# The first 26 and the last 40 microseconds of a layernorm–attention–SwiGLU kernel, put in another order

## Chip, cores and metric

The kernel runs on one core of a Trainium2 chip. The metric is the device time of one execution in microseconds (us). Times are given as the median of several runs; a profile is one execution more, taken by the hardware profiler, with a time of its own.

## What is computed

The input is x, 2048 rows of 512 numbers in float32. The reference, cut to what matters:

```python
xn = _layernorm(x, axis=-1)               # eps 1e-5
qkv = xn @ wqkv                           # H = 32 heads of Dh = 16
p = softmax(einsum(q, k) * Dh ** -0.5)    # 2048 x 2048 for each head
s = einsum(p, v) @ wo
b = (silu(xn @ w_gate) * (xn @ w_up)) @ w_down   # F = 1792
out = x + s * silu(b)
```

## The kernel before

**Precision.** A large product is made from three products: each operand is split into a rounded high part (a copy into the type fp32r) and the rest (a subtraction), and high·high, low·high and high·low are summed. So each operand costs a cast and a subtraction on its way, and each product three matmuls. Softmax weights times values alone run in plain float32.

**Opening and projections (L431 to L676).** The rows come in 4 blocks of 512 (`b`), each of 4 tiles of 128 rows (`t`). For one tile: `stats` (L501, L502) takes mean and variance, `rates` (L506 to L512) the reciprocal root, with one Newton step after ScalarE's square root, `norm` (L516) subtracts and multiplies into `xn`, and `turn_x` (L518 to L528) turns the tile by four transposes on TensorE into a bank `acc`, from which ScalarE copies the high part (L524) and VectorE makes the low one (L525). `load_w` and `split_w` (L461, L469, L470) bring a piece of wqkv and split it: ScalarE casts, GpSimd subtracts. In block 0 the four `value_tile`s come first (12 matmuls each, L538), then the eight `feature_tile`s (q and k, L536); in the later blocks the features come first. Before the first value tile stand: tile 0 in full, the four value weights' splits, then the statistics, rates and norms of the tiles 1 to 3 together. The list `slots` and the conditions on `n` in the loop after it set what is issued between the tiles. Each engine runs its own instructions in the order in which the program issues them.

**Attention (L740 to L777).** 32 units (`u`: 8 groups of 4 heads by 4 blocks of queries) of 8 steps each; the number of the step is `now`. In a step: 8 score matmuls, 4 exponentials on ScalarE (L749), and the value matmuls of the step before (L360). Between them `share` hands out a part of a queue of filler matmuls (L171): the whole feed-forward network of the 4 blocks (`ffn`), then the output projections (`project_out`): the one of block 3 with three of the four pieces of the attention output, then those of blocks 0, 1 and 2. They use the banks `bankx` and `banky`, each over 64 of the 128 rows of the array, and VectorE empties these two banks after each tile (for an output projection L330, L331); GpSimd then multiplies by the gate, adds x and stores (L332 to L334).

**Attention output.** `finish` normalises a unit; after every second group a turned piece `o2` goes to a scratch tensor in HBM (`o_d`, L382). `out_steps` plans, by `now` and by the length of the queue, when the pieces come back (`load_out`, L274), when they are split (`split_o`, L257, L258), and when the gates and rows of x are loaded (`load_gates`). The dictionary `stage` keeps what has been done; a projection of block b may start only when `(b, 3)` is in it, that is, when its last piece has been split. `load_gate` and `gate_rest` (L350, L351: four multiplications and four additions on VectorE) prepare the rows of block 3 in steps 248 and 251.

**The end (L778 to L801).** After the last values, block 3 of the last unit is normalised in two halves, turned, and split into `hi` and `lo`. `fill(total)` issues the 12 matmuls that remain of the projections (row tile number `end` = 11, into half of `score[0]`, L321). Then come four products with three matmuls each (L798) into the four banks of `outs`, a multiplication by the gate (L799), an addition (L800) and a store (L801) each.

Of the kernel before, what the change touches and what calls it, by code (L numbers as in the profile page):

```python
# [46 lines left out]
def tile_block(ctx: ExitStack, tc: tile.TileContext, x, wqkv, wo, w_gate, w_up, w_down, out):  # L47
# [237 lines left out]
    stage = {}  # L285
    splits = []

    def out_steps():
        for _ in range(min(2, len(splits))):
            b, c = splits.pop(0)  # L290
            split_o(lhs[b, c], parts_o[b, c])
            if c == DT - 1:
                stage[b, 3] = now
        for b in range(NB - 1):
# [10 lines left out]
            if (b, 1) in stage and (b, 5) not in stage and now > stage[b, 1]:  # L305
                splits.append((b, DT - 1))
                stage[b, 5] = now
            if len(queue) <= NB - 1 - b and (b, 4) not in stage:
                load_gates(b)
                stage[b, 4] = now  # L310

    def project_out(b, n=DT):
        catch_up()
        for j in range(NT):
            t = b * NT + j
            i = 0
            for c in range(n):
                for a, w in ((0, 0), (0, 1), (1, 0)):
                    lo, hi = lhs[b, c][a][:, j * P:(j + 1) * P], fx[:, w, c]
                    if t == end:  # L320
                        mm(score[0][:, 1], lo, hi, start=i == 0, stop=i == 3 * n - 1)  # L321
# [3 lines left out]
                    if i == 3 * n and n == DT:  # L325
                        y = two.tile([P, D], F32, tag="th", name="y")
                        if t == end:
                            act(y, score[0][:, 1], AF.Copy, scale=0.5)
# [3 lines left out]
                        pool.tensor_mul(y, y, gt[t])  # L332
                        pool.tensor_add(xr[t], y, xr[t])
                        (sp if t == end else pool).dma_start(out[rows[t]], xr[t])  # L334
# [66 lines left out]
    def fill(n):  # L401
        nonlocal given, left
        while n > 0 and queue and (queue[0][0] is None or (queue[0][0], 3) in stage):
# [25 lines left out]
    with ExitStack() as pro:  # L429
# [8 lines left out]

        def load_x(b):
            for t in range(NT):  # L440
                r = b * TB + t * P
                sp.dma_start(xin[:, t], x[r:r + P])

        load_x(0)
# [28 lines left out]
        for m in worder[:5]:  # L473
            load_w(m)
# [29 lines left out]
        def rates(first, last):  # L504
# [13 lines left out]
        def turn_x(b, t):  # L518
# [5 lines left out]
            nc.scalar.copy(hi, av)  # L524
            dve.tensor_sub(lo, av, hi.bitcast(F32))  # L525
# [4 lines left out]
        def project(pairs, xh, xl, tokens):  # L530
            ps = pps.tile([P, 512], F32, tag="ps", name="ps")
            n = 0
            for whi, wlo, c in pairs:
                for a, w in ((xh, whi), (xl, whi), (xh, wlo)):
# [41 lines left out]
        def value_tile(b, t):  # L576
            xh, xl = xt[b % 2]
            ps = project([(vh[:, c], vl[:, c], c) for c in range(DT)], xh, xl, slice(t * P, (t + 1) * P))
# [247 lines left out]
```

## Time and profile before

| | us |
|---|---|
| median of 3 runs | 1464.09 (1462.9 to 1464.17) |
| the profiled execution, its own time | 1465.16 |
| its span, first to last instruction | 1463.4 |
| TensorE busy with matmuls | 1440.6 |
| ScalarE busy | 1094.6 |
| VectorE busy | 536.0 |
| GpSimd busy | 91.2 |

The profile names engines PE (TensorE matmuls), PEld (its weight loads), DVE (VectorE), ACT (ScalarE), POOL (GpSimd) and SP (the queue that issues most DMAs). A row of the timeline has the start and the length in us, the engine, the line, the operation, the tiles written and read, their shapes and how often; in brackets, how long the engine was idle before it and what released it. A row of the windows view has a stretch, its length, the busy time of the engines, then the granted TensorE clock (1.00 is full speed), the share of time in which the DMA engines were busy, and what they moved in GB/s. Matmul ends are modelled, so the pitch from one start to the next is the safer measure.

### The profile page before, as it was taken

The page shows a single profiled execution, that of the slowest core. Times are in us where ns is not written, and L with a number is a line of the kernel's source. Part 1 is how long each engine was busy: PE and PEld are TensorE (multiplying, and loading weights), DVE is VectorE, ACT ScalarE, POOL GpSimd, SP SyncE. Part 2 cuts the span into 40 slices and gives each one's busy share as a digit, 9 for nine tenths or more (in the row PEclk, how much of TensorE's full clock was granted, in tenths as well). Part 3 has the DMA queues.
Part 4 walks back from the last instruction along what each step waited for, and adds up shares of the span by engine and source line. Part 5 has one row for each costly group of instructions (what it writes and reads, how often), then busy time and mean ns, then how long its engine had stood idle before and what let it go on. Part 6 is the DMA issues. An engine that isn't in the chain of part 4 may idle for free.

```text
span 1463.4 us, 26699 instructions
## 1 busy us (share of the span) xinstructions
PE 1440.6 (98%) x11213; PEld 803.8 (55%) x11213; DVE 536.0 (37%) x883; ACT 1094.6 (75%) x1218; POOL 91.2 (6%) x108
## 2 busy tenths in 40 slices
PE   7999999999999999999999999999999999999997
PEld 5777655555555555555555555555555555555553
DVE  5543343124333432244233423342334214334444
ACT  4433488788878887888788878887888778877773
POOL 3200200000000000000000000000000000000244
PEclk9999999999999999999999999999999999999999
DMA  7799652033273431143714401448144203313351
GB/s 254 267 288 296 166 120 61 12 88 88 69 173 79 92 77 34 45 103 81 166 42 108 99 12 40 101 94 182 35 98 107 55 12 69 93 52 127 114 193 73
DMA packets 130066, 155.94 MB, mean 107 GB/s; under 512 B 12764, under 2 KB 79324, under 8 KB 128916
## 3 DMA queue, kind: packets, MB, share of 16 engines
q1 hardware_dynamic: 124372, 131.17, 36.1%
q0 software_dynamic: 5280, 22.48, 4.1%
q8 instruction: 90, 1.47, 0.4%
q10 hardware_dynamic: 288, 0.52, 0.1%
q14 instruction: 36, 0.29, 0.1%
HBM read 111.66 MB, written 42.47 MB: 105 GB/s over the span
## 4 chain that ended last, share of the span: by engine, by line
PE 95%; DVE 2%; ACT 2%; DMA 1%; issue 1%; DVEq 0%; ACTq 0%
PE acc L360 32%; PE bankx L171 29%; PE score L747 20%; PE ps L536 5%; PE banky L171 5%; PE ps L538 3%; ACT pr L749 1%; DMA q_d<-parts 1%; PE acc L521 1%; DVE facc L350 0%; DMA facc<-in_A_x_dram 0%; DVE y L799 0%; DVE st L501 0%; DVE y L800 0%; PE score L798 0%
## 5 line engine op out<-in xcount | busy, mean ns | idle before, releaser
L749 ACT ACTIVATE pr<-score 128x1024 f32<-128x1024 f32 x1024 | 992.4, 1023 | 240.3 <-PE score L747 237.6
L360 PE MATMUL acc<-pr,vst 128*17 128x512 f32 x4096 | 490.0, 596 | 0.0
L747 PE MATMUL score<-qst,kst 50*128 50x512 f32 x2048 | 360.8, 424 | 2.8 <-ACT pr L749 2.0
L747 PEld LDWEIGHTS score<-qst,kst 50*128 50x128 f32 x2048 | 178.2, 185 | 273.1 <-ACT pr L749 235.6
L171 PE MATMUL bankx<-fx,guh 64*128 64x512 f32 x896 | 288.4, 392 | 0.0
L171 PE MATMUL banky<-fx,guh 64*128 64x512 f32 x896 | 288.3, 392 | 0.0
L360 PEld LDWEIGHTS acc<-pr,vst 128*17 128x17 f32 x4096 | 94.0, 96 | 236.5 <-issue 235.7
L199 DVE SCALAR_TENSOR_TENSOR ga<-th,bankx 128x512 f32<-128x512 f32 x56 | 38.5, 688 | 463.5 <-ACT th L198 463.5
L171 PEld LDWEIGHTS bankx<-fx,guh 64*128 64x128 f32 x896 | 165.8, 185 | 32.6 <-issue 0.3
L171 PE MATMUL bankx<-fx,gul 64*128 64x512 f32 x448 | 175.4, 391 | 0.0
L171 PE MATMUL banky<-fx,gul 64*128 64x512 f32 x448 | 175.3, 391 | 0.0
L171 PEld LDWEIGHTS banky<-fx,guh 64*128 64x128 f32 x896 | 165.7, 185 | 4.1
L171 PE MATMUL bankx<-wd,hh 64*128 64x512 f32 x672 | 165.8, 389 | 0.0
L171 PE MATMUL banky<-wd,hh 64*128 64x512 f32 x672 | 165.6, 388 | 0.0
L171 PEld LDWEIGHTS bankx<-wd,hh 64*128 64x128 f32 x672 | 124.0, 184 | 24.8
L171 PEld LDWEIGHTS banky<-wd,hh 64*128 64x128 f32 x672 | 124.0, 184 | 2.2
L171 PEld LDWEIGHTS bankx<-fx,gul 64*128 64x128 f32 x448 | 82.9, 185 | 17.5
L171 PEld LDWEIGHTS banky<-fx,gul 64*128 64x128 f32 x448 | 82.8, 185 | 1.8
L536 PE MATMUL ps<-xt,wh 128*128 128x512 f32 x256 | 80.9, 397 | 0.0
L131 DVE TENSOR_TENSOR gul<-gur,guh 128x1024 fp32r<-128x1024 f32 x56 | 68.6, 1225 | 2.1
L218 DVE COPY facc<-bankx 128x512 f32<-128x512 f32 x16 | 11.1, 692 | 131.0 <-PE banky L171 103.9
L382 POOL DMA_DIRECT2D o_d<-o x12 | 6.5, 545 | 820.7 <-DVE o L381 623.0
(138 smaller groups left out, 1050.5 us busy)
## 6 DMA issues: line engine op xcount, KB each, us to landing
fx<-xt_d SPq DMA_DIRECT2D x32, 512.0 KB
gur<-in_B_w_gate_dram SPq DMA_DIRECT2D x56, 256.0 KB
gur<-in_B_w_up_dram SPq DMA_DIRECT2D x56, 256.0 KB
wdr<-in_B_w_down_dram SPq DMA_DIRECT2D x56, 256.0 KB
kst<-k_d SPq DMA_DIRECT2D x192, 64.0 KB
qst<-q_d SPq DMA_DIRECT2D x192, 64.0 KB
xt_d<-xt POOLq DMA_DIRECT2D x8, 1024.0 KB, 6.2
q_d<-parts SPq DMA_DIRECT2D x16, 512.0 KB
```

The costliest lines, as they stand in the source:

```text
L131: dve.tensor_sub(lo, raw, hi.bitcast(F32))
L171: mm(bank, lhs[h], rhs[h], start=start, stop=stop)
L199: dve.scalar_tensor_tensor(ga, th, 1.0, bankx, op0=ALU.add, op1=ALU.mult)
L218: dve.tensor_copy(facc[:, t], bankx)
L360: mm(a[h * 32:h * 32 + DH + 1], v[:, kt % CT, h * (DH + 1):(h + 1) * (DH + 1)], probs[2 * i + h // 2][:, h % 2], start=kt == 0, stop=kt == ...
L382: (pool if g < NG - 1 else sp).dma_start(o_d[g // 2, b], o2)
L521: nc.tensor.transpose(a[:, c * P:(c + 1) * P], xn[t][:, c * P:(c + 1) * P], ident)
L536: mm(ps, w, a[:, c], start=n == 0, stop=n == 3 * DT - 1)
L538: mm(ps, a[:, c, tokens], w, start=n == 0, stop=n == 3 * DT - 1)
L747: mm(score[j][:, h], k[r, j, kc * P:(kc + 1) * P], q[r, j], start=True, stop=True)
L749: exps.append(act(pr, score[j], AF.Exp, scale=0.25))
```

## The change

Three places change; the matmuls of the 256 steps of attention stay as they are and in their order.

*Opening.* Twelve plain float32 matmuls of the identity with itself go to the bank `acc[1]` before any other work on TensorE. The loads come in the order x0, w8, x1, w9, w10, w11, x2, x3, w0 (before: x0 to x3, then w8 to w11 and w0). `rates` uses scalar operands: where three products of two tensors stood, each row tile has one operation with two scalar operands and one with one. The splits of w8 and w9 are issued ahead of the copies of tile 0, the statistics of tile 1 between its two copies, and tile 1 is normalised by itself. Value tile 0 takes all eight products with the high weights first, then two of the four with the low weights, then the transposes of row tile 1, then the other two; the other value tiles of block 0 take the products with `xl` last. The tiles 2 and 3 are normalised and turned after value tile 1. The loads of block 1 are issued one slot later.

*Attention output.* For the blocks 1 and 2 the last piece no longer goes through HBM: `finish` splits `o2` at once into slots of `wd` or `hh`. A counter `ready` takes the place of `(b, 3)`. For block 0 the last piece's split goes to the front of the list.

*End.* `fill(total)` stands ahead of the last normalisation; row tile 11 goes to `bankx`, and its evacuation (ScalarE) and its GpSimd work are issued after the first half of the last unit. Row tile 10 is stored from the SP queue instead of GpSimd's. `outs[2]` is `banky` instead of the other half of `score[1]`; the second low part is issued after the second product; all additions are on VectorE, and the stores alternate between the SP and the ScalarE queue.

```diff
+    ready = [0] * NB
...
             split_o(lhs[b, c], parts_o[b, c])
-            if c == DT - 1:
-                stage[b, 3] = now
+            ready[b] += 1
...
-            if b in stage and (b, 1) not in stage and now > (u0 + b) * steps:
+            if b in stage and not b and (b, 1) not in stage and now > (u0 + b) * steps:
...
-                splits.append((b, DT - 1))
+                splits.insert(0, (b, DT - 1))
...
+    def store_out(t, y):
+        pool.tensor_mul(y, y, gt[t])
+        pool.tensor_add(xr[t], y, xr[t])
+        (pool if t < end - 1 else sp).dma_start(out[rows[t]], xr[t])
...
-                        mm(score[0][:, 1], lo, hi, start=i == 0, stop=i == 3 * n - 1)
+                        mm(bankx, lo, hi, start=i == 0, stop=i == 3 * n - 1)
...
-                            act(y, score[0][:, 1], AF.Copy, scale=0.5)
+                            after.append(partial(act, y, bankx, AF.Copy, scale=0.5))
+                            after.append(partial(store_out, t, y))
...
-            (pool if g < NG - 1 else sp).dma_start(o_d[g // 2, b], o2)
+            if g < NG - 1 or not b:
+                (pool if g < NG - 1 else sp).dma_start(o_d[g // 2, b], o2)
+            else:
+                whole = (wd, hh)[b - 1].rearrange("p f j t -> p (f j) t")
+                lhs[b, DT - 1] = whole[:, 2 * (DT - 1)], whole[:, 2 * DT - 1]
+                split_o(lhs[b, DT - 1], o2)
+                ready[b] += 1
...
-        load_x(0)
...
-        for m in worder[:5]:
-            load_w(m)
+
+        for _ in range(12):
+            mm(acc[1][:, :P], ident, ident, start=True, stop=True)
+        for kind, i in ((load_tile, 0), (load_w, 8), (load_tile, 1), (load_w, 9), (load_w, 10), (load_w, 11),
+                        (load_tile, 2), (load_tile, 3), (load_w, 0)):
+            kind(i)
...
-            dve.tensor_mul(n, r, r)
-            dve.tensor_mul(n, n, v)
+            each = [[i[:, t:t + 1] for i in (rs, nw, ve)] for t in range(first, last)]
+            for rt, n1, vt1 in each:
+                dve.tensor_scalar(n1, vt1, rt, rt, op0=ALU.mult, op1=ALU.mult)
             dve.tensor_scalar(n, n, -0.5, 1.5, op0=ALU.mult, op1=ALU.add)
-            dve.tensor_mul(r, r, n)
+            for rt, n1, _ in each:
+                dve.tensor_scalar(rt, n1, rt, None, op0=ALU.mult)
...
             nc.scalar.copy(hi, av)
+            if between:
+                between()
             dve.tensor_sub(lo, av, hi.bitcast(F32))
...
+        def later(n):
+            if n == 3:
+                for t in (2, 3):
+                    stats(t)
+            else:
+                stats(1)
+
         stats(0)
         rates(0, 1)
+        split_w(8, pool)
         norm(0)
-        turn_x(0, 0)
-        for m in worder[:DT]:
+        split_w(9, pool)
+        turn_x(0, 0, partial(later, 1))
+        for m in (10, 11):
             split_w(m, pool)
-        for t in range(1, NT):
-            stats(t)
-        rates(1, NT)
+        rates(1, 2)
         norm(1)
-        norm(2)
...
+            order = then = None
+            if b == 0:
+                parts = (slice(0, 2), slice(2, 3)) if t == 0 else (slice(0, 3, 2), slice(1, 2))
+                order = [(i, part) for part in parts for i in range(DT)]
+                then = partial(turn_x, 0, 1, partial(later, 3)) if t == 0 else None
...
-                if n == 1 and more:
+                if n == (1 if b else 2) and more:
                     load_x(b + 1)
...
-                if b == 0 and n in (1, 2):
-                    turn_x(0, n + 1)
+                if b == 0 and n == 1:
+                    rates(2, NT)
+                    norm(2)
+                    norm(3)
                 made = make(b, i)
+                if b == 0 and n == 1:
+                    for t in (2, 3):
+                        turn_x(0, t)
...
-                if b == 0 and n == 0:
-                    turn_x(0, 1)
-                    norm(3)
...
-    outs = (score[0][:, 0], score[1][:, 0], score[1][:, 1], acc[units % 2])
+    outs = (score[0][:, 0], score[1][:, 0], banky, acc[units % 2])
...
+    fill(total)
+    assert not queue and given == total
     turned = []
...
         nc.scalar.copy(hi[:, cols[n]], turned[n][:, :half])
-    low(1)
-    fill(total)
-    assert not queue and given == total
+        catch_up()
...
+    def gated(t):
+        dve.scalar_tensor_tensor(y[t], outs[t], 0.5, gate[t], op0=ALU.mult, op1=ALU.mult)
+
+    def stored(t):
+        dve.tensor_add(y[t], y[t], facc[:, t])
+        (sp, nc.scalar)[t % 2].dma_start(out[rows[(NB - 1) * NT + t]], y[t])
+
     for t, ps in enumerate(outs):
...
-        dve.scalar_tensor_tensor(y[t], ps, 0.5, gate[t], op0=ALU.mult, op1=ALU.mult)
-        (pool if t < 2 else dve).tensor_add(y[t], y[t], facc[:, t])
-        (nc.scalar if t < 2 else sp).dma_start(out[rows[(NB - 1) * NT + t]], y[t])
+        if t == 1:
+            low(1)
+        if t < NT - 1:
+            gated(t)
+    stored(0)
+    stored(1)
+    gated(3)
+    stored(2)
+    stored(3)
```

More of the change, by code (lines that the diff above doesn't have):

```diff
@@ L402, in fill @@
         nonlocal given, left
-        while n > 0 and queue and (queue[0][0] is None or (queue[0][0], 3) in stage):
+        while n > 0 and queue and (queue[0][0] is None or ready[queue[0][0]] == DT):
             left = next(queue[0][1])
@@ L528, in turn_x, with project @@
                     pool.dma_start(xt_d[b, j], xt[b % 2][j].bitcast(F32))
-        def project(pairs, xh, xl, tokens):
+        def project(pairs, xh, xl, tokens, order=None, then=None):
             ps = pps.tile([P, 512], F32, tag="ps", name="ps")
             n = 0
-            for whi, wlo, c in pairs:
-                for a, w in ((xh, whi), (xl, whi), (xh, wlo)):
+            terms = [((xh, whi), (xl, whi), (xh, wlo)) for whi, wlo, _ in pairs]
+            for i, part in order or [(i, slice(0, 3)) for i in range(DT)]:
+                c = pairs[i][2]
+                if then and n == 10:
+                    then()
+                for a, w in terms[i][part]:
                     if tokens is None:
@@ L577, in value_tile @@
             xh, xl = xt[b % 2]
[L578 removed]
+            order = then = None
[3 more added lines that the diff above has]
+                then = partial(turn_x, 0, 1, partial(later, 3)) if t == 0 else None
+            ps = project([(vh[:, c], vl[:, c], c) for c in range(DT)], xh, xl, slice(t * P, (t + 1) * P), order, then)
             nc.scalar.copy(vt5[:, :, t, :, :DH], ps.rearrange("p (g h d) -> p g h d", g=NG, h=4))
```

11 lines of the change are left out of this document (5 added, 6 removed).

## The prediction

> **What bounds the kernel now.** I read the page first, then the windows of the opening, then the timeline at both ends.
>
> ```profile
> PE 1440.6 (98%) x11213; PEld 803.8 (55%) x11213; DVE 536.0 (37%) x883; ACT 1094.6 (75%) x1218; POOL 91.2 (6%) x108
> ...
> PE 95%; DVE 2%; ACT 2%; DMA 1%; issue 1%; DVEq 0%; ACTq 0%
> ...
> 0.00:8.79 8.79, 1.09 (x4) 0.71 (x4) 4.31 (x21) 2.84 (x6) 0.71 (x6) 1.00 0.76 253
> 25.57:50.00 24.43, 24.43 (x117) 19.63 (x116) 14.10 (x25) 13.28 (x26) 9.37 (x9) 1.00 0.73 257
> ```
>
> TensorE is 95% of the chain that ended last, so only its empty or slow time can be won, and the order of its 256 attention steps is unchanged. It has three weak places. In the first 8.79 us it works 1.09 us; from 25.57 us, where the first feature tile begins, it works without a gap. So whatever brings that point forward moves all that follows. The other two places are a stall near 1431 us and the tail.
>
> The execution profiled took 1465.16 us, 1.76 more than its span of 1463.4. It lies 1.07 above the median of 1464.09. I work the differences out on the profiled one and take them off the median. About 0.2% (2.9 us) is what a measurement of this kernel can tell from no change.
>
> **Opening.**
>
> ```profile
> 1.03 0.29 POOL masks.py:199 TENSOR_SCALAR_AFFINE_SELECT ident<-ident 128x128 f32<-128x128 f32 x1
> ...
> 4.42 0.15 DVE L506 TENSOR_SCALAR ve<-mv 128x1 f32<-128x1 f32 x1
> 4.61 0.20 ACT L507 ACTIVATE nw<-ve 128x1 f32<-128x1 f32 x1 [2.37 <-DVE ve L506]
> ...
> 5.82 0.55 DVE L516 TENSOR_SCALAR xn<-facc,mv,rs 128x512 f32<-128x512 f32 x1
> ...
> 6.51 1.09 PE L521 MATMUL acc<-ident,xn 128*128 128x128 f32 x4 [6.51 <-DVE xn L516]
> 7.64 0.58 ACT L524 CAST xt<-acc 128x512 fp32r<-128x512 f32 x1 [2.82 <-PE acc L521]
> 8.12 2.58 ACT L469 CAST vh<-wraw 128x512 fp32r<-128x512 f32 x4
> ...
> 8.82 5.00 POOL L470 TENSOR_TENSOR vl<-wraw,vh 128x512 fp32r<-128x512 f32 x4 [7.50 <-ACT vh L469]
> ...
> 10.76 1.05 PE L538 MATMUL ps<-vh,xt 128*128 128x512 f32 x2
> ...
> 11.39 1.22 DVE L506 TENSOR_SCALAR ve<-mv 128x3 f32<-128x3 f32 x1
> ...
> 11.61 0.63 PE L538 MATMUL ps<-vl,xt 128*128 128x512 f32 x1
> ...
> 18.16 0.39 PE L538 MATMUL ps<-vl,xt 128*128 128x512 f32 x1
> ...
> 19.10 0.62 PE L538 MATMUL ps<-vh,xt 128*128 128x512 f32 x2
> ...
> 25.80 0.62 PE L536 MATMUL ps<-xt,wh 128*128 128x512 f32 x2
> ...
> 162.04 1.07 PE L668 MATMUL low<-row,sel 1*64 1x512 f32 x2
> ```
>
> Two matmuls take 1.05 us at 10.76 but 0.62 at 19.10, single ones 0.63 and 0.39: by the differences the pitch is 0.42 at first and 0.23 later. So the array starts at about half speed, though the clock column shows 1.00 there. Value tile 0 is held to GpSimd's four subtractions (5.00 us, 8.82 to 13.82), which begin only after the copy of tile 0 on ScalarE.
>
> *Identity matmuls.* The trace has no plain float32 128x128 matmul. Below, the four transposes: 1.09 us, 0.21 to 0.27 each. Above, L668, a plain float32 product of 512 columns, issued as two matmuls: 1.07 for the pair at full speed. A quarter of it for 128 columns is 0.27, times 0.42/0.23 at the slow clock 0.49. I take 0.49, the nearest in kind; twelve are 5.9 us. They start at about 1.4, after the identity (1.03 + 0.29), and end near 7.3; ends kept are 4.0 (transposes) and 14.2 (twelve whole pairs).
>
> *Splits first.* By 253 GB/s over the first 8.79 us a load of 262 KB takes some 1.0 us, so w8, second in the new order, is there well before ScalarE ends the square root (4.61 + 0.20). Its cast then runs 4.8 to 5.5, and GpSimd's first subtraction, 1.25 long, from about 5.5, 3.3 earlier than before. But `norm(0)` is due only at 5.6 (from 4.61 to 5.82 lie the root and five small operations, some 0.2 each, and one goes). Look at L506: 0.15 us at 4.42, but 1.22 at 11.39, while GpSimd subtracted. A VectorE operation of this kind waits for GpSimd's. So I let `norm(0)` end at 7.35 instead of 6.37. [...]
>
> From there, with the rows' durations: transposes to 8.0; high copy 8.1 to 8.7; VectorE's statistics of tile 1 beside it (some 0.9, estimated from the 0.55 of a `norm`) and the low part to 9.4; casts of w10, w11 to 9.9, GpSimd to 11.9; the square root of tile 1 waits for the casts (9.9), and its `norm` again for GpSimd, so xn(1) is ready at 12.5. Value tile 0 ends at 13.5, tile 1 (8 matmuls, then 4) at 16.5. The rates of tiles 2 and 3 (some ten small operations, 2 us) and two norms put their transposes at 17 to 18; tile 2 starts at 18.2, and two tiles of 12 matmuls, 0.23 each, end at 23.7. Before, the feature tile started at 25.57, with its second pair at 25.80. **Opening: 1.9 us less**, if the array runs at full speed from about 9; at half speed until 14 it is 0.5 less; without both waits behind GpSimd 3.0.
>
> The later loads hide behind the value tiles; the block 1 loads, now one slot later, still wait only for the last norm. Without that cover each 262 KB would cost about 1 us.
>
> **The stall near 1431 us.**
>
> ```profile
> 1417.36 1.91 PE L360 MATMUL acc<-pr,vst 128*17 128x512 f32 x16
> ...
> 1422.18 1.91 PE L360 MATMUL acc<-pr,vst 128*17 128x512 f32 x16
> ...
> 1422.85 0.42 DVE L257 CAST hh<-hh 128x512 fp32r<-128x512 f32 x1
> ...
> 1423.03 1.38 POOL L332 TENSOR_TENSOR y<-y,gates 128x512 f32<-128x512 f32 x1 [5.65 <-DMA gates<-g_d]
> 1423.30 1.65 DVE L258 TENSOR_TENSOR hh<-hh 128x512 fp32r<-128x512 f32 x1
> ...
> 1427.94 1.91 PE L360 MATMUL acc<-pr,vst 128*17 128x512 f32 x16
> ...
> 1429.78 0.74 PE L747 MATMUL score<-qst,kst 50*128 50x512 f32 x4
> ...
> 1431.29 0.68 DVE L330 TENSOR_SCALAR y<-bankx 128x512 f32<-128x512 f32 x1
> 1432.02 0.49 PE L171 MATMUL bankx<-fx,hh 64*128 64x512 f32 x1 [1.51 <-DVE y L330]
> ...
> 1432.82 0.49 PE L171 MATMUL banky<-fx,hh 64*128 64x512 f32 x1 [0.30 <-DVE y L331]
> ...
> 1434.00:1435.00 1.00, 1.00 (x8) 0.81 (x5) 0.00 (x0) 0.00 (x0) 0.92 (x2) 0.50 0.00 0
> ...
> 1446.55 1.91 PE L360 MATMUL acc<-pr,vst 128*17 128x512 f32 x16
> ```
>
> The last piece of block 2 is split here (0.42 and 1.65, the latter stretched by GpSimd); behind it on VectorE stand `gate_rest`'s eight operations, and behind those L330, which frees the bank. TensorE has nothing from 1430.52 (1429.78 + 0.74) to 1432.02, and little to 1432.82: 2.3 us; then its clock falls to 0.50. The steps show the price: 4.82 from 1417.36 and 5.76 from 1422.18 (these two have 6 and 12 filler matmuls), but 18.61 for the three from 1427.94 to 1446.55 (6, 6 and 12 fillers: 4.82 + 4.82 + 5.76 = 15.4 at that rate). So 3.2 are lost, 2.3 by the stall and some 0.9 to 1.0 by the clock.
>
> The change moves the split to `finish`, near 1410, where its two operations lie between evacuations; without that room they would cost 1.1 again. But the two GpSimd operations now collide with `gate_rest` in place of the split: eight operations of 0.68 like L330, plus some 2.5 of waits for two GpSimd operations of 1.25, end at 1430.8 when begun at 1422.9, instead of 1431.29. **0.5 less** (nothing to 1.1). TensorE's thin stretch shrinks from 2.3 to about 1.7 us. Whether that still lowers the clock no row decides; with a quarter gone, and the gap moved by all that was won before it, I take it that it doesn't: **1.0 less** (nothing to 1.7, which allows 0.7 for what the next steps hid). What remains late is still L330 behind `gate_rest`. The HBM trips that vanish were hidden.
>
> **The tail.**
>
> ```profile
> 1448.39 3.06 PE L321 MATMUL score<-fx,hh 128*128 128x512 f32 x12
> ...
> 1451.95 0.40 ACT L790 CAST rh<-o 128x256 fp32r<-128x256 f32 x1 [1.26 <-DVE o L789]
> 1452.26 0.59 ACT L328 ACTIVATE y<-score 128x512 f32<-128x512 f32 x1
> ...
> 1452.90 0.72 PE L798 MATMUL score<-fx,rh 128*128 128x512 f32 x2 [1.46 <-ACT y L328]
> ...
> 1453.96 1.34 DVE L799 SCALAR_TENSOR_TENSOR y<-score,hh 128x512 f32<-128x512 f32 x2 [1.15 <-PE score L798]
> ...
> 1455.35 0.73 PE L798 MATMUL score<-fx,rh 128*128 128x512 f32 x2 [0.78 <-DVE y L799]
> ...
> 1457.08 1.51 DVE L800 TENSOR_TENSOR y<-y,facc 128x512 f32<-128x512 f32 x1
> ...
> ...
> 1459.22 0.69 DVE L800 TENSOR_TENSOR y<-y,facc 128x512 f32<-128x512 f32 x1
> ```
>
> The first product waits for ScalarE's L328, which shares `score[0]`, the third (1455.35) for a multiplication on `score[1]`; both waits go. The last values and the 12 filler matmuls stay, so product 0 starts at 1451.2 and ends near 1452.1. Then VectorE binds: gate 0 to 1452.9; the second low part, behind GpSimd's multiplication for tile 11, to 1453.8; gates 1 and 2 to 1455.2; then two additions, a gate and two additions, 0.67 each, end at 1458.5. Before, the last ended at 1459.91. **1.4 less** (0.8 to 1.8). ScalarE's evacuation of tile 11 now stands ahead of the second cast (1451.95) and delays it 0.3, beneath gate 0; tile 10's store from SP waits in front of nothing that is ready. The last store leaves ScalarE's queue instead of SP's; I price that at nothing.
>
> Sum: 1.9 + 0.5 + 1.0 + 1.4 = 4.8. 1464.09 - 4.8 = **1459.3**.
>
> **Rivals.**
>
> *Better, no waits behind GpSimd (0.12).* The opening gives 3.0, the stall 1.1, the clock 1.7, the tail 1.8: 7.6, so 1456.5. For: the new one-number operations may not need what the 128x3 one did. Against: `norm` itself stays 512 wide.
>
> *The array stays slow (0.15).* Twelve products of an identity may not count as work, or the clock may fall again in the gaps between transposes and tile 0. Then the opening gives 0.5, and the clock near 1431 falls as before: 0.5 + 0.5 + 1.4 = 2.4, so 1461.7. For: before, TensorE worked from 8.79 and was still slow at 10.76. [...] No row here shows identity matmuls.
>
> *The loads take the gain back (0.08).* The projections move as much as the memory gives:
>
> ```profile
> ACT parts L569 <- DMA q_d<-parts: 11.8, 4, 3.9
> ```
>
> If those stores cannot come earlier, the opening's 1.9 is lost: 1461.1. Against: the DMA share is 0.73 from 25.57 to 50, and TensorE has no gap there.
>
> *Slower (0.06).* The identity matmuls cost a pair of L668 each, whatever their width: 12 x 1.07 = 12.8, to 14.2. The first transposes wait for them, 6.2 us later than in my sum less what later slack absorbs (some 1.0, the wait for xn(1)): the feature tile starts at 23.7 + 6.9 - 1.0 = 29.6, 4.0 late. With the stall lost and clock as before (0) and the tail's 1.0, the end is 3.0 later: 1467.1. It decides once the twelve end after some 11 us: by then the opening's 1.9 and the tail's and stall's 1.9 are used up.
>
> **Chances.** Forecast 0.59, better 0.12, slow array 0.15, loads 0.08, slower 0.06. The forecast's own bounds are 1457.0 to 1461.5. The range 1456.0 to 1462.2 leaves out the slower rival and the outer parts of the others. Faster by over 0.2% is below 1461.16: most of the forecast, all of the better case, about a third of the next two: 0.75. Within: 0.19. Slower: 0.06.
>
> **What would show it.** Right: the first L536 matmul near 23.7; twelve identity matmuls ending by 7.4; a `norm` stretched over 1 us by GpSimd; no 0.50 clock near 1430; the first L798 product 1.7 earlier against the last values, the last addition 1.4. Wrong: a pitch of 0.42 in value tile 1, a gap of TensorE in the projections that before had none, or full-speed starts with the feature tile still after 25.

## The result, and the profile after

| | before | after |
|---|---|---|
| median, us | 1464.13 (1462.31 to 1465.4, 14 runs) | 1459.33 (1457.87 to 1463.2, 14 runs) |
| ratio, 95% interval | | 0.9971 (0.9963 to 0.998) |
| profiled execution: own time, span | 1465.16, 1463.4 | 1459.36, 1457.6 |

The median fell by 4.8 us, the profiled execution by 5.8. The total is what was forecast; its parts are not. First the page of after: engines, and the chain that ended last.

```profile
PE 1441.6 (99%) x11237; PEld 806.6 (55%) x11237; DVE 537.7 (37%) x905; ACT 1094.5 (75%) x1219; POOL 88.2 (6%) x105
...
PE 95%; ACT 2%; DVE 1%; DMA 1%; issue 0%; DVEq 0%; ACTq 0%
```

TensorE still carries 95% of the chain; what was won is idle or slow time of its own. The timeline of the opening after:

```profile
1.38 5.39 PE L486 MATMUL acc<-ident 128*128 128x128 f32 x24 [1.38 <-POOL ident masks.py:199]
...
5.38 1.27 POOL L481 TENSOR_TENSOR vl<-wraw,vh 128x512 fp32r<-128x512 f32 x1 [4.06 <-ACT vh L480]
5.77 1.16 DVE L533 TENSOR_SCALAR xn<-facc,mv,rs 128x512 f32<-128x512 f32 x1
6.17 0.62 ACT L480 CAST vh<-wraw 128x512 fp32r<-128x512 f32 x1 [0.87 <-DMA wraw<-in_A_wqkv_dram]
...
9.04 1.90 PE L563 MATMUL ps<-vh,xt 128*128 128x512 f32 x7 [0.23 <-DVE ve L521]
...
10.38 1.29 DVE L533 TENSOR_SCALAR xn<-facc,mv,rs 128x512 f32<-128x512 f32 x1
...
17.29 0.50 PE L563 MATMUL ps<-vh,xt 128*128 128x512 f32 x1 [0.22 <-ACT xt L541]
...
22.98 0.63 PE L561 MATMUL ps<-xt,wh 128*128 128x512 f32 x2
```

Each of the twelve identity products is two matmuls (x24), 0.45 us a product, and all end at 6.77. Both norms are stretched to 1.16 and 1.29 beside a GpSimd subtraction (0.55 at 5.82 in before, where none ran). The seven matmuls from 9.04 take 1.90, a pitch of about 0.25, so the array is at full speed there. The first feature tile starts at 22.98; before it started at 25.80: **2.8 us earlier**, not 1.9.

ScalarE's copies of the feature tiles show that it doesn't stay so. The 28th one, before and then after:

```profile
137.01 0.58 ACT L569 CAST parts<-ps 128x512 fp32r<-128x512 f32 x1 [3.92 <-DMA q_d<-parts]
```

```profile
135.64 0.58 ACT L600 CAST parts<-ps 128x512 fp32r<-128x512 f32 x1 [5.32 <-DMA q_d<-parts]
```

In both, ScalarE waits for an earlier tile's store to HBM before it may overwrite `parts`; after, it waits 1.4 longer. The lead falls from 2.78 to 1.38 at this instruction, and 1.3 of it lives through attention.

The stall, on the timeline of after, and two stretches of its windows:

```profile
1421.55 0.68 DVE L354 SCALAR_TENSOR_TENSOR facc<-facc,hh 128x512 f32<-128x512 f32 x1
...
1422.27 1.65 DVE L355 TENSOR_TENSOR facc<-facc,last 128x512 f32<-128x512 f32 x1
...
1423.85 1.78 DVE L354 SCALAR_TENSOR_TENSOR facc<-facc,hh 128x512 f32<-128x512 f32 x1
...
1428.92 0.68 DVE L336 TENSOR_SCALAR y<-bankx 128x512 f32<-128x512 f32 x1
...
1429.66 0.50 PE L171 MATMUL bankx<-fx,hh 64*128 64x512 f32 x1 [0.45 <-DVE y L336]
```

```profile
1429.90:1433.31 3.41, 3.12 (x24) 1.67 (x27) 0.51 (x1) 2.00 (x4) 2.57 (x2) 1.00 0.01 4
1433.31:1436.72 3.41, 3.39 (x30) 1.73 (x22) 0.15 (x1) 2.84 (x4) 0.58 (x1) 1.00 0.20 77
```

`gate_rest` still runs into two GpSimd operations (1.64 from 1421.73 and 1.63 from 1423.45; beside them 1.65 and 1.78 for operations of 0.68), and the release of the bank (L336, formerly L330) comes 2.37 earlier than before, 1.07 of it beyond the lead that was there. The clock stays at 1.00. Last, the tail:

```profile
1442.59 1.91 PE L364 MATMUL acc<-pr,vst 128*17 128x512 f32 x16
...
1447.32 0.64 PE L844 MATMUL score<-fx,rh 128*128 128x512 f32 x2
...
1448.26 1.29 POOL L313 TENSOR_TENSOR y<-y,gates 128x512 f32<-128x512 f32 x1 [1.25 <-ACT y L155]
...
1448.83 1.00 DVE L821 TENSOR_TENSOR rl<-o,rh 128x256 fp32r<-128x256 f32 x1
...
1451.03 1.28 DVE L838 TENSOR_TENSOR y<-y,facc 128x512 f32<-128x512 f32 x2
...
1452.24 0.68 DVE L835 SCALAR_TENSOR_TENSOR y<-acc,wd 128x512 f32<-128x512 f32 x1
...
1452.84 1.28 DVE L838 TENSOR_TENSOR y<-y,facc 128x512 f32<-128x512 f32 x2
```

No product waits for a bank. The second low part takes 1.00 beside GpSimd's 1.29 from 1448.26 (the first 0.51), as forecast, and the last addition ends at 1454.12 (before 1459.91).

To see where time goes in each experiment, I compare the start of the same instruction in two traces. Each entry is "this kernel minus the kernel before" in us: the first, 27th and 32nd copy of a feature tile, the first exponential of steps 0, 253 and 255, the end of the span.

| | 1st | 27th | 32nd | step 0 | step 253 | step 255 | end |
|---|---|---|---|---|---|---|---|
| after | -2.81 | -2.78 | -1.38 | -1.32 | -1.29 | -3.95 | -5.83 |
| opening alone | -1.84 | -1.81 | -0.62 | -0.45 | +0.32 | +0.04 | +0.04 |
| attention output alone | +0.06 | +0.06 | +0.11 | -1.34 | -1.10 | -3.73 | -3.73 |
| attention output and end | +0.12 | +0.12 | +0.56 | +0.62 | +0.63 | -2.03 | -3.91 |
| after, no identity products | -0.80 | -0.77 | -0.21 | -0.15 | -0.27 | -2.92 | -4.79 |
| after, four `parts` buffers | -1.84 | -1.82 | -2.51 | -2.63 | -2.74 | -5.40 | -7.27 |
| before, four `parts` buffers | +0.22 | +0.24 | -0.46 | -0.39 | -0.41 | -0.39 | -0.39 |
| after, w8 split on VectorE | -3.29 | -3.27 | -1.71 | -1.66 | -1.80 | -4.46 | -6.35 |
| after, `gate_rest` spread | -2.32 | -2.32 | -1.18 | -0.81 | -0.84 | -4.55 | -6.42 |
| after, `norm(0)` issued first | -1.80 | -1.80 | -0.64 | -0.86 | -0.05 | -2.70 | -4.58 |
| after, three more identity products | -2.23 | -2.20 | -1.73 | -1.73 | -1.74 | -4.39 | -6.28 |
| best | -2.71 | -2.69 | -3.39 | -4.12 | -4.02 | -7.73 | -9.60 |
| best, w8 split on VectorE | -2.13 | -2.13 | -2.83 | -2.78 | -2.63 | -6.34 | -8.17 |

Each row is one profiled execution against one. In the seven rows with the new opening and three `parts` buffers, 0.5 to 1.6 of the lead is lost between the 27th and the 32nd tile; in the four rows with four buffers 0.7 is gained there. The jump of the third row at step 0 is no gain of that kernel but a stretch of slow clock that before had (0.50 from 164.14 to 167.55) and its execution didn't (1.00 from 163.07 to 166.48); more on that below.

### The profile page after: what moved, and what is told of

Read it like the earlier page. It is cut to its first block, busy times and chain, and to the rows that moved or that the text cites. A ratio compares the mean times of both kernels' runs of the same rounds, so it can differ in the third digit from the quotient of the medians.

```text
span 1457.6 us, 26766 instructions
## 1 busy us (share of the span) xinstructions
PE 1441.6 (99%) x11237; PEld 806.6 (55%) x11237; DVE 537.7 (37%) x905; ACT 1094.5 (75%) x1219; POOL 88.2 (6%) x105
## 4 chain that ended last, share of the span: by engine, by line
PE 95%; ACT 2%; DVE 1%; DMA 1%; issue 0%; DVEq 0%; ACTq 0%
PE acc L364 32%; PE bankx L171 29%; PE score L785 20%; PE ps L561 6%; PE banky L171 4%; PE ps L563 3%; ACT pr L787 1%; DMA q_d<-parts 1%; PE acc L538 0%; DVE facc L354 0%; PE bankx L326 0%; DMA facc<-in_A_x_dram 0%; DVE y L835 0%; DVE xn L533 0%; DVE y L838 0%
## 5 line engine op out<-in xcount | busy, mean ns | idle before, releaser
L600 ACT CAST parts<-ps 128x512 fp32r<-128x512 f32 x32 | 18.7, 585 | 52.0 <-PE ps L561 24.4
```

The costliest lines, as they stand in the source:

```text
L600: nc.scalar.copy(parts[:, 0], ps)
```

## The experiments

**Theory.** The opening brings the feature tile forward, and the stores of the parts take half of it back; the direct split ends the stall and with it the half clock near 1434; the tail adds its own. **Rival 1:** the loss at 135 us is chance, and the opening is worth its 2.8. **Rival 2:** the half clock has nothing to do with the stall, and the gain from step 253 to 255 comes from elsewhere.

**1. The opening alone** (all lines of the diff from `load_tile` to the transposes in the loop of slots, nothing else).

```diff
+        for _ in range(12):
+            mm(acc[1][:, :P], ident, ident, start=True, stop=True)
...
+        split_w(8, pool)
         norm(0)
+        split_w(9, pool)
...
```

> The opening alone, with the attention output and the end of before. My account, from the two traces: the first feature tile starts 2.8 us earlier, but the wait of ScalarE for the stores of parts near 136 us grows from 3.9 to 5.3 and gives 1.4 of it back, so 1.4 less in all, about 1462.7 beside 1464.1. Rival, the opening counts in full and the 1.4 was an accident of one execution: 2.8 less, 1461.3, with the 28th feature tile 2.8 earlier too. Rival, the loads take all of it back: no difference. The half clock near 1434 us, of which before had 3.4 us, should be there again if the stall brings it, since the stall of 2.3 us is unchanged.

Measured: 1461.97 (1460.67 to 1467.34, 11 runs), ratio 0.9995 (0.9985 to 1.0004). The median is 1.8 below that of its own runs of before (1463.74), but the interval of the ratio includes no change. In the profile the lead of 1.8 is gone in two places (table): 1.2 at the stores of the parts, and 0.9 from there to step 253. The 0.9 is lost at the start of attention: TensorE waits 2.55 us there (0.83 before), released at the branch `tc.If(fast < 1)`, and then the clock is at half from 169.65 to 173.07 (before: from 164.14 to 167.55). From step 253 to the end it gains 0.3, so the stall is there as before. And two new things, in windows laid on the clock's own changes:

```profile
5.81:9.23 3.42, 1.96 (x11) 1.22 (x11) 2.62 (x5) 2.08 (x5) 2.18 (x3) 1.00 1.01 346
9.23:12.64 3.41, 3.41 (x9) 2.64 (x9) 3.04 (x8) 0.17 (x2) 2.35 (x2) 0.50 1.07 290
...
1429.18:1432.59 3.41, 1.90 (x17) 0.55 (x9) 3.23 (x6) 2.83 (x3) 0.00 (x0) 1.00 0.21 77
1432.59:1436.00 3.41, 3.22 (x15) 2.30 (x15) 0.49 (x1) 0.00 (x0) 2.54 (x2) 0.50 0.00 0
```

The array rose early (clock 1.00 from 5.81), worked 1.96 of 3.41 us, and fell back to half for exactly the next 3.41. At the stall the same happens after 1.90 of 3.41.

**2. The attention output alone** (`ready`, `out_steps`, the split in `finish`).

```diff
+                split_o(lhs[b, DT - 1], o2)
+                ready[b] += 1
...
-        while n > 0 and queue and (queue[0][0] is None or (queue[0][0], 3) in stage):
+        while n > 0 and queue and (queue[0][0] is None or ready[queue[0][0]] == DT):
```

> The attention output alone: the last pieces of blocks 1 and 2 are split straight from o2, opening and end as before. My account: VectorE's L330 behind gate_rest comes 1.1 us earlier (the split's 0.42 and 0.69), the stall near 1431 shrinks from 2.3 to 1.2. If the shorter stall is what keeps the clock up, there is no half clock near 1434 and the last steps gain 2.6 together; if the clock hangs on where the stall falls in time, it may be there still and the gain is 1.1. In time 1463.0, or 1461.5 where an execution of before has the half clock.

Measured: 1462.48 (1460.76 to 1462.94, 11 runs), ratio 0.9991 (0.9982 to 1.0): 1.3 by the medians, at the edge of what these runs can tell from no change. In the profile -1.10 at step 253 and -3.73 at step 255: the 2.6 of stall and clock belong to this part. The window of the stall:

```profile
1429.43:1432.84 3.41, 2.66 (x20) 1.75 (x24) 1.08 (x2) 1.98 (x3) 2.05 (x2) 1.00 0.24 77
1432.84:1436.25 3.41, 3.41 (x30) 1.66 (x25) 0.00 (x0) 2.84 (x4) 1.09 (x2) 1.00 0.20 77
```

2.66 busy, and the clock holds. Before, for comparison:

```profile
1430.49:1433.90 3.41, 1.60 (x13) 1.10 (x13) 2.14 (x4) 1.77 (x2) 1.04 (x1) 1.00 0.23 77
1433.90:1437.31 3.41, 3.41 (x17) 1.24 (x17) 0.00 (x0) 1.94 (x2) 2.09 (x3) 0.50 0.12 46
```

All three profiled kernels with the old split (before, 1 and 11) fall to half here, after 1.60, 1.90 and 1.89; none of the eleven with the direct split does. Rival 2 is out for the profiled executions.

**3. Without the identity products.**

```diff
-        for _ in range(12):
-            mm(acc[1][:, :P], ident, ident, start=True, stop=True)
```

> The changed kernel without the twelve identity matmuls. If they are what brings the full clock to 6.5 us, the array is slow until about 10.4 or 13.9 here, the value tiles 0 and 1 take some 0.2 us more for each matmul, and the first feature tile comes 1.0 to 2.0 later than in the changed kernel. If the loads and stores near 136 us are a floor, the 28th feature tile comes no later or at most 0.6 later, and the time is that of the changed kernel, 1459.3 to 1460. Rival, no floor: the 1.0 to 2.0 stand at the end, 1460.3 to 1461.3. Rival, the identity matmuls do nothing but delay: equal or up to 0.5 faster.

Measured: 1460.38 (1458.13 to 1460.81, 9 runs), ratio 0.9975 (0.9965 to 0.9985). The first feature tile comes 2.0 later than in after (table: -0.80 for -2.81), so most of the opening's gain is the identity's; but only 1.2 is left of it at the 32nd tile. I had expected 0.6 at most at the 28th tile, and 1460 at most in time, so the stores take back less of a lead than I thought. The two ratios' intervals overlap: what the identity products bring at the end is under what the medians can separate.

**4. Four buffers for `parts`.**

```diff
-        p3 = pro.enter_context(tc.tile_pool(name="p3", bufs=3))
+        p3 = pro.enter_context(tc.tile_pool(name="p3", bufs=4))
```

> The changed kernel with four buffers of parts instead of three. If the 1.4 us are lost because ScalarE waits for the store that frees the oldest of three buffers, a fourth lets it go on: no gap of TensorE near 135 us, the 28th feature tile 2.8 earlier than before, the time 1.4 less than the changed kernel's, about 1457.9. Rival, the stores themselves are the floor and the wait comes back one tile later: the same gap, the same time, 1459.3.

Measured: 1457.12 (1455.95 to 1457.92, 5 runs), ratio 0.9955 (0.9941 to 0.9968): the median is 2.2 below that of after, and the intervals of the two ratios overlap by 0.0005. The copies of the 28th and 29th tile:

```profile
132.99 0.59 ACT L600 CAST parts<-ps 128x512 fp32r<-128x512 f32 x1 [1.71 <-issue]
135.73 0.59 ACT L600 CAST parts<-ps 128x512 fp32r<-128x512 f32 x1 [1.65 <-PE ps L561]
```

No wait for a store: the lead grows from 1.82 to 2.51 there, where in after 1.4 was lost. This although this execution's clock fell back in the opening as in experiment 1 (0.50 from 9.47 to 12.88; lead 1.84 at first). Rival 1 is out: the stores took it.

The next place takes back some more. This execution has no half clock near 164 us (1.00 from 162 to 170), which gave 1.45 in experiment 2 (from +0.11 to -1.34), but between the 32nd tile and step 0 it gains only 0.12. The first score product of attention stands

```profile
166.80 0.97 PE L785 MATMUL score<-qst,kst 50*128 50x512 f32 x4 [2.21 <-PEq L717]
```

L717 is the branch `tc.If(fast < 1)`; before, TensorE waited 0.83 us at this place, and for ScalarE. What holds the branch stays open.

**5. `gate_rest` spread over four steps**, one row tile in each of steps 251 to 254.

```diff
-    def gate_rest():
-        for t in range(NT):
+    def gate_rest(t):
+        if 0 <= t < NT:
...
-            if now == (units - 1) * steps + 3:
-                gate_rest()
+            gate_rest(now - (units - 1) * steps - 3)
```

> The changed kernel with gate_rest spread over the steps 251 to 254, one row tile in each, instead of all four in step 251. In the changed kernel TensorE still has about 1.2 us without work near 1429 us, while L336 waits behind the eight operations. If that is the whole of the stall, it goes: the steps 253 to 255 come 1.2 earlier against step 252, the time is 1.2 less than the changed kernel's, about 1458.1. Rival, the operations only move to where they delay the evacuations of the next tiles: no gain, 1459.3.

Measured: 1458.21 (1457.47 to 1458.74, 5 runs), ratio 0.9966 (0.9952 to 0.9979): by the medians 1.1 less than after, 1.2 expected, with intervals that overlap. Now the second projection tile is emptied as soon as it is there:

```profile
1426.80 0.69 DVE L336 TENSOR_SCALAR y<-bankx 128x512 f32<-128x512 f32 x1 [2.43 <-PE banky L171]
```

VectorE waits for TensorE instead of the other way round, and from step 253 to 255 this kernel gains 3.7 on before (from -0.84 to -4.55), 1.05 more than after. So what was left of the stall was indeed `gate_rest` standing ahead of L336.

**6. `norm(0)` issued ahead of `split_w(8)`** (one run).

```diff
-        split_w(8, pool)
         norm(0)
+        split_w(8, pool)
```

> The changed kernel with the first norm issued before the split of w8, so that on ScalarE, VectorE and GpSimd nothing of that split runs beside it. Nothing else moves. If norm is stretched by GpSimd's subtraction, it takes 0.55 instead of 1.16 here and xn of tile 0 is ready near 6.3 instead of 6.93; the subtraction starts when it did or is itself held until then. Since the identity matmuls end only near 6.8, the transposes start at 6.8 instead of 7.0, and the feature tile comes at most 0.2 earlier. If its length had another cause, norm takes 1.1 to 1.2 again.

Measured: 1460.58; `norm(0)` is as long as before the edit:

```profile
5.77 1.16 DVE L533 TENSOR_SCALAR xn<-facc,mv,rs 128x512 f32<-128x512 f32 x1
```

A miss of the experiment, not of either theory: the two lines go to different engines, and nothing moved: `norm(0)` stands at 5.77 and GpSimd's subtraction at 5.38, both as in after. Experiment 9 asks again.

**7. Three more identity products after the first transposes.**

```diff
+            for _ in range(3 if b == t == 0 else 0):
+                mm(acc[1][:, :P], ident, ident, start=True, stop=True)
```

> The changed kernel with three more identity matmuls behind the transposes of row tile 0, where TensorE otherwise has nothing from about 7.6 to 8.3 us. Two of the profiles with the new opening fell back to half clock at 9.2 and 9.5 us and rose again 3.4 later, and their feature tile came 1.0 later than where it did not fall. If that gap is why it falls, it doesn't fall here, in any execution: first feature tile 2.8 before that of the kernel before, no execution at a mean clock of 0.995 or 0.996, and the slow ones of the changed kernel (1461.2 to 1463.2) are missing. The median falls by 0 to 0.7 to 1458.6 to 1459.3. Rival, identity matmuls do not keep the clock, only their number at the start does: it falls back as often, and three matmuls at half clock cost 0.7.

Measured: 1458.9 (1458.59 to 1459.31, 8 runs), ratio 0.997 (0.996 to 0.9981). The median hardly moves, but the spread does: 4 of after's 14 runs lie above 1461, none of these 8 above 1459.31. If the 4 fell at random among these 22 runs, the 8 would have none of them one time in seven, so this is a hint at the gap ahead of tile 0 and no more. The first feature tile leads by 2.2, not by the 2.8 expected.

**8. Best: edits 4, 5 and 7 together.**

> The changed kernel with the fourth buffer of parts, gate_rest spread over four steps, and the three identity matmuls behind the first transposes. If the three gains are independent: 2.2 by the buffers, 1.2 by the spreading, 0 to 0.7 by the clock, so 1455.2 to 1455.9 beside 1459.3, and 0.55 to 0.6% less than before. If the fourth buffer already holds all that there is to win behind the opening, the clock's part vanishes and it is 1456.

Measured: **1456.05** (1455.56 to 1456.28, 5 runs), ratio 0.9953 (0.9939 to 0.9967): 7.5 below its own runs of before (1463.55), where after is 4.8 below its own. This is the second case of the expectation: the clock's part does not show. Every run lies below every run of after; the intervals of the two ratios overlap by 0.0004. Near 164 us this execution has no half clock (1.00 from 162 to 170). That shows as 0.7 in the table (from -3.39 to -4.12) and not as the 1.45 of experiment 2, because TensorE then waits 1.64 us for the same branch as in experiment 4.

**9. The subtraction of w8 on VectorE, after `norm(0)`** (one run).

```diff
-        split_w(8, pool)
         norm(0)
+        split_w(8)
```

> The changed kernel, but the subtraction of w8 runs on VectorE, issued after norm(0), where the changed kernel has it on GpSimd: no GpSimd operation stands beside norm(0). If norm(0) is held by GpSimd (1.16 us at 5.77 with a GpSimd subtraction of 1.27 from 5.38), it takes 0.55, as before, and starts in the same place. If the price lies in the new scalar operands or in the earlier place, it keeps 1.1 to 1.2. The other rival: the second norm, which the changed kernel has at 10.38 with 1.29, keeps over 1.1 in either case, since GpSimd still subtracts the other three pieces beside it.

Measured: 1458.81, and on the timeline:

```profile
5.93 0.55 DVE L533 TENSOR_SCALAR xn<-facc,mv,rs 128x512 f32<-128x512 f32 x1
```

With no GpSimd operation beside it (the first begins at 7.06) the norm takes 0.55. The second one, beside GpSimd, keeps 1.28. So the wait behind GpSimd is shown, and it cost `norm(0)` 0.6.

**10. The attention output and the end, with the old opening.**

> The changed kernel with the old opening: attention output and end alone. If the three parts add up, its profiled marks stand as before up to step 1012, gain about 2.65 from there to step 1020 if the execution profiled before the change had a half-clock stretch there and this one has none, and 1.9 in the tail; by medians 1.0 to 1.3 for the attention output (1462.5 alone) and 1.9 for the tail, so 1460.6 to 1461.2. If the tail's gain needs the other parts, the median stays near 1462.5.

Measured: 1459.93 (1459.62 to 1461.66, 10 runs), ratio 0.9973 (0.9964 to 0.9983). In the profile the parts add up: -2.66 from step 253 to 255 (the expectation's 1012 and 1020 count exponentials, four to a step), and -1.88 from there to the end, as in after. At the median they do not: 4.5 below its own runs of before (1464.4), where 1.3 and 1.9 make 3.2. And the ratio is that of after (0.9971) within its interval: at the median the opening's share is too small to measure.

**11. The kernel before with four `parts` buffers** (edit 4 alone).

> The kernel before with one more buffer in the pool of the parts (4 for 3), nothing else. If the stores of the parts bind at the 28th feature tile in the kernel before as well (ScalarE waits there 3.9 us for a store, 1.1 of it more than the steady pace), the marks behind it move up by 0.8 to 1.4 and the median falls by 0.7 to 1.4, so 1462.4 to 1463.1. If only the earlier opening runs into the stores, nothing moves: within 0.3 of before.

Measured: 1463.43 (1461.46 to 1464.77, 10 runs), ratio 0.9992 (0.9982 to 1.0001), in time no measurable change; in the profile 0.70 is gained between the 27th and 32nd tile. So the stores bind before too, a little; the earlier opening runs deeper into them.

**12. Best with edit 9 as well.**

> All four edits on the changed kernel: four parts buffers, one row tile of gate_rest per step, three identity matmuls after the first transposes, and the subtraction of w8 on VectorE after norm(0). Without the last edit the median was 1456.05. With it the first feature tile starts some 0.5 earlier than in the changed kernel (as in the run with that edit alone); with four buffers this reaches the end: 1455.4 to 1455.8. If a store or a load gives it back, 1456.0 to 1456.3. If the earlier first transposes only widen the gap in which the clock falls back, some runs lie above 1457.

Measured: 1456.56 (1456.06 to 1458.87, 5 runs), ratio 0.995 (0.9936 to 0.9963): no better than 8, where up to 0.65 less was expected. Its execution shows why the profile of an opening must be read with care:

```profile
7.64 0.62 ACT L480 CAST vh<-wraw 128x512 fp32r<-128x512 f32 x1 [2.33 <-DMA wraw<-in_A_wqkv_dram]
```

The same cast stood at 6.17 in after. Over the ten kernels with the new order of loads w9 is cast at 6.17 to 6.36 in four and at 7.02 to 7.64 in six, whatever the edit, and the first feature tile leads by 1.8 to 2.3 in the late ones and by 2.7 to 3.3 in the early ones (apart from the one without identity products). (Of the late ones, the 1.8 are those whose clock fell back as well.) After's 2.8 is a lucky draw.

One of the five runs lies at 1458.87, so the three products of edit 7 do not exclude long runs. There is no profile of it.

## Why the prediction was right, and where it was not

The total was right (1459.3 forecast, 1459.33 measured). In the profile every term came out at or above its forecast: 2.8 + 1.07 + 1.6 + 1.9 = 7.4 instead of 4.8. A loss that I held unlikely took 1.4 of that, and the profiled execution of before was about 1 longer than its median. So that the match is so close is luck: errors cancel. At the median the opening's 1.9 is not shown: without it (experiment 10) the kernel is 4.5 below its own runs of before, with it 4.8.

*Opening, 1.9 forecast.* The prediction took 25.57 for the start of the first feature tile before. There the last product of value tile 3 still runs, as this row of before shows; the feature tile starts at 25.80:

```profile
25.57 0.40 PE L538 MATMUL ps<-vl,xt 128*128 128x512 f32 x1
```

So the start forecast at 23.7 was 2.1 earlier, not 1.9. The order is as forecast, each step somewhat early: identity products to 6.77 (7.3), `norm(0)` to 6.93 (7.35), tile 2 at 17.29 (18.2). In the profile that makes 2.8, in executions where w9 lands late 1.8 to 2.3. The sum assumed that w9's cast follows without a wait; that wait is the widest unknown of the opening that the profiles show. No row of before shows the condition that the array runs at full speed from about 9; in after the clock changes at 6.54 and the seven matmuls from 9.04 take 1.90, in experiment 1 seven from 9.03 take 3.21. The wait behind GpSimd, taken from one small operation (1.22 for 0.15), is shown by experiment 9: `norm(0)` takes 0.55 without a GpSimd operation beside it, 1.16 with one.

*The step that failed is "Against: the DMA share is 0.73 from 25.57 to 50, and TensorE has no gap there".* With it I put the loads rival at 0.08. The evidence was from the wrong place: the stores bind at 132 to 137 us, and the quoted row of waits (3.9 us, the longest of four) was that instruction. Where a line that otherwise waits 1.7 waits 3.9, there is the point at which a lead is paid back. The stores took 1.4 of 2.8 here, 1.2 of 1.8 in experiment 1, 0.5 of 2.2 in experiment 7, and nothing with a fourth buffer (experiment 4). So about half of this rival came true, with a share that differs between executions. (Its time by the prediction's own terms is 1464.09 - 2.9 = 1461.2, not 1461.1.)

*Stall, 0.5 forecast, 1.07 measured.* The mechanism is right (the split gone, two GpSimd operations in its place, `gate_rest` still ahead of the bank). The size: eight operations took 7.37 from 1421.55 to 1428.92, and I had 7.94. Two waits cost 2.07, not 2.5, and back to back the operations start 0.66 apart, not 0.68.

*Clock, 1.0 forecast.* From step 253 to 255 the profile gains 2.66, of which 1.07 is the stall: 1.6 for the clock, within the range given (0 to 1.7). The term was too small: most of the 0.7 that I allowed for what the next steps hid came on top of the 1.0. That the clock would hold was a guess then. Measured are 1.60 us of matmuls in the 3.41 us ahead of the half clock of before, and 3.12 in after's 3.41 us from 1429.90, with 1.00 behind them.

*Tail, 1.4 forecast, 1.9 measured.* The first product stands 1.62 earlier against the last values (forecast 1.7). The rest is a mis-sized term: from the first pair of additions to the end I took five operations of 0.67; they start about 0.6 apart and take 3.09 in all (1451.03 to 1454.12) instead of 3.35; the gates ahead of them ended 0.2 sooner too.

*The frame.* 5.8 in the profile and 4.8 at the median differ because the profiled execution of before had two stretches of half clock (near 164 and 1434). Of the 25 runs of before beside experiments 1 to 4, 7 have a mean clock of 0.999 and take 1461.96 to 1462.46, 12 have 0.998 and take 1463.48 to 1464.16, 5 have 0.997 and take 1465.10 to 1465.73 (one more, 0.996, 1464.42): steps of about 1.5, which I read as one half stretch each. The two profiled executions without any half clock between opening and tail (experiments 2 and 8) have 0.999 too, so in 7 of the 25 runs even the old stall seems to have brought none. The profiled execution, 1465.16, belongs to the last group, the median to the middle. So of the two half stretches that the profile shows, a usual execution has one; experiment 2 gives 1.3 at the median for stall and clock together, where its profile shows 2.6 and the forecast had 1.5.

*Rivals.* "Slow array" asked whether products of an identity count as work: with them the array is fast by 5.2 to 7.1 us in every profile, without them or with the old opening at 12.9 to 14.6. But its second condition, the fall in the gap between transposes and tile 0, happened in 3 of the 9 profiles with them (in none of the three with edit 7). The "slower" rival's price (12.8 for the twelve) is out: 5.4.

## What to carry to other kernels

A lead won early is worth only what the next shared buffer or store lets through: look along the whole run for the line whose wait is longest against its usual one, and give it a buffer more before winning time ahead of it. The stall on TensorE cost twice in before: 2.3 us with little or no work, then 3.41 us at clock 0.50; a few matmuls that compute nothing, put into a gap, may be cheaper than the stretch at half clock (experiment 7, with three of them, hints at it and does not settle it). And VectorE's wait for GpSimd was undone by moving the work to another engine (0.55, experiment 9), not by swapping two lines that go to different engines (1.16, experiment 6).

## What the runs showed of the hardware

*Where the clock changed.* In before it changes at 13.95, 164.14, 167.55, 1433.90 and 1437.31; in after at 6.54, 163.55 and 166.96; in experiment 1 at 5.81, 9.23, 12.64, 169.65, 173.07, 1432.59 and 1436.00. In each of these three executions the changes lie whole multiples of 3.413 us apart (from 13.95 to 1433.90 it is 1419.95, 416 times that). A window is here one such stretch, laid off from the changes of its execution. The windows ahead of a fall are not idle. Of those in the openings, one of experiment 4 and one of experiment 5 stand closest to each other; here two windows of 4, then two of 5:

```profile
6.05:9.47 3.42, 2.10 (x11) 1.32 (x11) 2.38 (x5) 2.30 (x4) 2.28 (x3) 1.00 0.99 335
9.47:12.88 3.41, 3.41 (x11) 2.52 (x10) 2.95 (x8) 0.25 (x2) 2.09 (x2) 0.50 1.10 298
```

```profile
7.09:10.50 3.41, 2.23 (x10) 1.52 (x11) 2.02 (x8) 2.24 (x5) 2.37 (x2) 1.00 1.10 344
10.50:13.91 3.41, 2.64 (x14) 1.58 (x13) 3.30 (x7) 0.98 (x2) 1.39 (x2) 1.00 0.88 241
```

In these two the next window is at half speed behind 2.10 us of matmuls, and isn't behind 2.23. The first windows of full speed in the nine openings with identity products are ordered alike (half behind 1.64, 1.96 and 2.10; not behind 2.23, 2.25, 2.29, 2.51 and more), and so are those of the stall (half behind 1.60, 1.89 and 1.90; not behind 2.66 and more). The windows lie elsewhere in each execution: those first ones begin at 5.21 to 7.09 us. That one and the same gap costs only itself when it is split between two windows is my estimate from this; no run shows it by itself.

*Busy time alone does not sort them.* In experiment 1 the clock holds behind a window of the projections with less, 1.88:

```profile
135.52:138.93 3.41, 1.88 (x10) 1.01 (x10) 0.69 (x1) 1.99 (x4) 0.00 (x0) 1.00 0.66 252
138.93:142.35 3.42, 3.42 (x16) 2.78 (x15) 0.98 (x2) 1.26 (x3) 0.00 (x0) 1.00 0.83 307
```

And near 164 us nine of the fourteen profiled executions fall to half after a window that is busy throughout (before):

```profile
160.73:164.14 3.41, 3.41 (x11) 1.24 (x10) 0.54 (x1) 1.18 (x2) 0.12 (x1) 1.00 1.03 249
164.14:167.55 3.41, 3.41 (x9) 2.64 (x10) 0.00 (x0) 2.03 (x2) 1.98 (x4) 0.50 0.79 175
```

In that one stand the products of a single row, L668 and L669, from 162.04 to 164.03. In all nine that fall there, these 2.0 us lie whole in the window just before. In the other five a border between two windows divides them, with at most 1.87 us in one window (experiment 4). So in these fourteen the half clock near 164 us goes with the place of the border, and no edit here earned its absence in experiments 2, 4 and 8. (In 1 and 6 the clock falls 5 us later, after windows with 0.86 and 1.25 us of matmuls, behind the wait for the branch.)

In the window of 1.88 stand only matmuls over all 128 rows, at the stall many over 50 or 64. But in the opening the clock fell behind 2.10 us of products over all 128 rows (identity, transposes, value tile 0). No experiment varied the rows, and what sets these places apart was not shown.
